# A fused sliding-window attention and mixture-of-experts kernel: one layout of the keys' blocks and its masks against another, with copies and routing steps on other engines

## The chip, the cores and the metric

The kernel runs on one core of one Trainium2 chip. The metric is the device time of one execution in microseconds (us). The kernel before was timed three times: median 500.73 us, from 499.25 to 502.19.

## What is computed

Attention first: batch 4, 8 heads, 768 positions, head size 64. A query sees the 4 first keys of its sequence (the "sinks") and the keys up to 127 positions behind it. Its result, 3072 rows of 512, goes through a mixture of experts: each row takes its best of 4 groups, then its best of that group's 4 experts, and gets that expert's output (512 to 1024, ReLU, 1024 to 512) times two softmax weights. Shortened:

```python
rel = pos[:, None] - pos[None, :]
keep = (pos[None, :] < n_sink) | ((rel >= 0) & (rel < window))     # 4 and 128
a = softmax(where(keep, q @ k.T / sqrt(64), -1e9)) ;  x = rows(a @ v)   # [3072, 512]
g = argmax(x @ w_group) ;  e = argmax(x @ w_expert[g])
out = softmax(x @ w_group)[g] * softmax(x @ w_expert[g])[e] * (relu(x @ w1[g, e]) @ w2[g, e])
```

## The kernel before, in words

*Tiles.* The attention works on 24 tiles of 128 queries (`NI`), six for each batch element (`NT`); all 8 heads of a tile in two groups `g` of four. The main loop (L1209) is a pipeline: iteration `i` makes the scores of tile `i`, weighs the values of tile `a = i-1`, and brings tile `b = i-2` into its natural layout, norms it and makes its routing logits. After the loop come the experts (to 497 us), which the change doesn't touch.

*One tile.* `scores` (L746): TensorE (PE) multiplies each half of 64 queries (on its own half of the partitions) with three blocks of 64 keys, its own and the two before it, each with the 4 sink keys, into the PSUM tile `ps`. With a window of 128 the oldest and the newest block are both needed in part, and in complementary parts: above the diagonal the one, below it the other. The kernel "folds" them: `maxima` (L768) copies by a mask `selu` (a predicated copy) the oldest block's scores over the places of the newest block that lie in the future, so that two blocks of 64 remain, and then runs four instructions of 128x136 per group on VectorE (DVE) that scale, add the mask `msk` and take the row's maximum (`sm`, `st`). `exps` (L783) makes the exponentials `pt` on ScalarE (ACT). `trans` (L797) transposes them on PE into the PSUM tile `tp` (`tp2` in the code), 8 instructions a group, each group in its own columns (`256 * g`); `evac` (L806) copies a group with one ACT instruction of 128x512 to `pw`; `halves` (L812) takes the fold apart again on GpSimd (POOL): two products of the folded quarter with two triangular 0/1 masks `tri`. `values` (L848) multiplies with the value blocks into `po`. The sinks go apart: `sink_copy` (POOL), `sink_t` (PE), `sink_evac` (ACT, `spT`), `sink_values` (PE). Tiles with `t = 0` (the first of a batch element) have no older keys, and neither fold nor masks.

*The two tiles behind.* `out_evac` (L857) copies `po` to `xT` (ACT), `natural` (L861) transposes it into `nat`, other columns of the same PSUM tile (so the trace calls it `po` too), `norm` (L873) divides by the row sums (`xt<-po,rc` on DVE) and writes the tile to memory. `logits` (L867) multiplies `xT` with the routers' weights, into spare columns of the first `ps` tile, and `norm_logits` (L883) takes them out (`lw` on DVE): only then can the next `scores` write there.

*Routing.* `route_batch` (L356) turns the logits of a batch of six tiles (`BATCHES`) into tables, in some 20 steps; each `yield` is a step's end, `yield "pe"` comes ahead of matmuls, `yield "rd"` ahead of reading their result. The main loop takes steps between the attention's instructions through `unit`, `UNITS` (L59) says how many a tile: four in tile 7, seven in tile 8, six in most others, so the batches of tiles 0 to 5, 6 to 11 and 12 to 17 are worked off in the attention, the last one behind it. `on` is POOL in the attention, DVE behind it.

*Order.* Every instruction goes through `_Eng`, which keeps each engine's instructions in the order written. So each trace row bears that helper's line, L105, and rows are told apart by their tile names. PE's weight loads (PEld) run beside its matmuls. The experts' weights are split into two parts in the gaps of the attention (`whi` on ACT, `wlo` on DVE).

```python
L772  v.copy_predicated(psb[g][:, :, SW + NSK:3 * BW], selu..., psb[g][:, :, NSK:BW])      # maxima, t > 0
L776  v.tensor_tensor_reduce(sm[:, k], psb[g][:, k, BW + s:3 * BW + s], msk[:, min(t, 2), s:SW + s], ...)
L809  nc.scalar.copy(pw[:, 0:8]..., tp2[:, :, 256 * g:256 * (g + 1)]...)                  # evac
L816  nc.gpsimd.tensor_tensor(pw[:, 8 * k:8 * k + 4], pw[:, 0:4], tri[:, k, None, :]...)  # halves, k = 1, 0
```

Of the kernel before, what the change touches and what calls it, by code (L numbers as in the profile page):

```python
# [37 lines left out]
SW = 2 * BW  # L38
# [96 lines left out]
def moe_attention(tc, kqT, vN, vS, nsw, wgx, w1, w2, out):  # L135
    nc = Pinned(tc)
    v = nc.vector
    with ExitStack() as top, ExitStack() as att:
# [117 lines left out]
        isu = gp.tile([P, D], F32, name="xg")  # L256
        v.tensor_scalar(isu, dq, 0.0, None, ALU.is_lt)
        rel = gp.tile([P, D], F32, name="xg")
        v.scalar_tensor_tensor(rel, isu, float(P), dq, ALU.mult, ALU.add)
        msk = const([P, 3, MW], F32, "msk")  # L260
        mb, ms, mc = msk[:, :, NSK:BW], msk[:, :, BW:BW + NSK], msk[:, :, BW + NSK:SW]
# [3 lines left out]
        v.tensor_scalar(m4[:, 0, ::SW // NSK], col[:, None, 0:NSK].to_broadcast([P, 2, NSK]), 0.0, NEG, ALU.is_ge, ALU.mult)  # L265
        selu = const([P, D], I32, "selu")
        v.tensor_scalar(selu, dq, 0.0, None, ALU.is_lt)
        dqd = const([P, D], F32, "dqd")
        v.tensor_scalar(dqd, dq, float(D), None, ALU.add)
# [10 lines left out]
        v.tensor_scalar(mc[:, 2], rel, win, NEG, ALU.is_ge, ALU.mult)  # L280
        v.tensor_scalar(snk, col[:, 0:D], nsk, NEG, ALU.is_lt, ALU.mult)
        v.tensor_scalar(mb[:, 2], dqd, win, NEG, ALU.is_ge, ALU.mult)
        v.scalar_tensor_tensor(mc[:, 0], isu, NEG, mc[:, 2], ALU.mult, ALU.add)
# [5 lines left out]
        tri = const([P, 2, D], F32, "tri")  # L289

        def other_masks():
            v.tensor_scalar(tri[:, 0], dq, 0.0, None, ALU.is_le)
            v.tensor_scalar(tri[:, 1], dq, 0.0, None, ALU.is_gt)
            v.tensor_copy(m4[:, 2, ::BW // NSK], m4[:, 0, ::BW // NSK])
            v.tensor_copy(msk[:, 1], msk[:, 2])
            v.tensor_tensor(snk[0:D], snk[0:D], isu[0:D], ALU.mult)
            v.tensor_tensor(mc[0:D, 1], mc[0:D, 1], snk[0:D], ALU.add)
# [58 lines left out]
        def route_batch(i0, nb, lt, wk, pt, tab, na, pick=None):  # L356
# [19 lines left out]
            v.tensor_tensor(d, lv, wide(m), ALU.subtract)  # L376
            yield
# [10 lines left out]
            v.tensor_tensor(oh.rearrange("p n (g e) -> p n g e", g=G), o5[:, :, 1:],  # L388
# [26 lines left out]
            v.tensor_tensor(runb, runb, rs, ALU.add)  # L415
# [18 lines left out]
            v.tensor_tensor(m, og, s5[:, :, 1:], ALU.mult)  # L434
            yield
# [13 lines left out]
            for j0 in range(0, nb, 3):  # L449
# [5 lines left out]
                v.tensor_tensor(af[:, j0:j1], oh[:, j0:j1, :, None].to_broadcast([P, w, NE, na]),  # L455
# [290 lines left out]
        def scores(i, g):  # L746
            t = i % NT
            if g == 0:
                env[i] = e = {}
                e["pt"] = wk.tile([P, HP, 2, 2, BW], F32, name="pt", bufs=2)  # L750
# [17 lines left out]
        def maxima(i, g, between=lambda k: None):  # L768
            t = i % NT
            e = env[i]  # L770
            if t:
                v.copy_predicated(psb[g][:, :, SW + NSK:3 * BW], selu[:, None, :].to_broadcast([P, 4, D]), psb[g][:, :, NSK:BW])  # L772
            between(0)
            e["sm", g] = sm = wk.tile([P, 4, SW], F32, name="sm", bufs=2)
            for k in range(4):
                h, s = head(g, k), k % 2 * NSK  # L776
                v.tensor_tensor_reduce(
                    sm[:, k], psb[g][:, k, BW + s:3 * BW + s], msk[:, min(t, 2), s:SW + s], -0.125, 3.0e38,
                    ALU.add, ALU.min, e["st"][:, h:h + 1])
                if k % 2:  # L780
                    between(k)

        def exps(i, g, ks=range(4)):  # L783
            e = env[i]
            for k in ks:
                h = head(g, k)
                nc.scalar.activation(e["pt"][:, 2 * g + k // 2, :, k % 2], e["sm", g][:, k].rearrange("p (b k) -> p b k", b=2),
# [8 lines left out]

        def trans(i, g):  # L797
            pt = env[i]["pt"].rearrange("p m b l x -> p m b (l x)")
            for j in range(2):
                for k in range(2):  # L800
                    o = 256 * g + (2 * k + j) * D
                    for f in range(2):
                        r = slice(f * D, (f + 1) * D)
                        nc.tensor.transpose(tp2[:, f, o:o + D], pt[r, 2 * g + j, 1 - k, NSK:SW - NSK], ident[r, r])
# [13 lines left out]

        def sink_copy(i):
            src = env[i]["pt"].rearrange("p m b l x -> p m (b l x)")[:, :, SW - NSK:SW + NSK]  # L820
# [3 lines left out]
        def sink_t(i):  # L824
            for f in range(2):
                r = slice(f * D, (f + 1) * D)
                nc.tensor.transpose(tp2[:, f, 0:D], sp[i % 2][r], ident[r, r])

        def sink_evac(i):
            env[i]["spT"] = spT = wk.tile([P, P], F32, name="spT", bufs=2)  # L830
            nc.scalar.copy(spT.rearrange("p (f q) -> p f q", f=2), tp2[:, :, 0:D])
# [82 lines left out]
        def routing(k, kinds=(None, "pe", "rd")):  # L914
            while k > 0:
                if not rb or not have.issuperset(rb[0][0]):
                    return False
                kind = rb[0][2] if isinstance(rb[0][2], str) else None
                if kind not in kinds or (kind == "pe" and state["clk"] < state["at"]):
# [283 lines left out]
        def unit(k):  # L1203
            if quota[0] > 0 and routing(1, (None,)):
# [4 lines left out]
        for i in range(NI + 2):  # L1209
# [15 lines left out]
            if mid:  # L1225
                evac(a, 0)
# [4 lines left out]
            if live:  # L1231
# [4 lines left out]
                warm(FILL[i] if i < len(FILL) else 0, tp2[:, 0, 256:448])  # L1236
            if mid:
                sink_copy(a)
                halves(a, 0)
# [12 lines left out]
            if mid:  # L1252
                evac(a, 1)
# [3 lines left out]
            if mid and not live:  # L1257
                halves(a, 1)
# [12 lines left out]
            if live:  # L1271
                maxima(i, 1, unit)
# [346 lines left out]
```

## Time and profile before

| what | value |
|---|---|
| median of three runs | 500.73 us (499.25 to 502.19) |
| the profiled execution | 499.12 us; its span 497.3 us |
| busy, share of the span | PE 466.5 us (94%), PEld 396.2 (80%), DVE 347.0 (70%), ACT 326.1 (66%), POOL 170.3 (34%) |
| chain that ended last, by engine | PE 65%, DVE 11%, ACT 9%, issue 8%, POOL 4%, DMA 2% |
| of it, by tile | PE `po` 29%, PE `ph` 29%, ACT `pt` 5%, PE `tp` 4%, PE `ps` 3%, POOL `pw` 2% |

The span runs from the first instruction to the last; the time holds a little more, what lies around it. Busy time counts an engine's instructions, and a busy engine need not be the one that all wait for. The chain is followed back from the last instruction to whatever released each. `po`, `tp` and `ps` are the attention's PSUM tiles (`po` and `ph` are the experts' as well), `pt` its exponentials, `pw` its transposed weights. The shares are means over two parts with different limits, the attention and the experts, so stretches have to be read apart.

### The profile page before, as it was taken

What the parts mean: (1) busy time and instruction counts of PE and PEld (TensorE: products, weight loads), DVE (VectorE), ACT (ScalarE), POOL (GpSimd) and SP (SyncE); (2) the same over time, 40 slices, a digit from 0 to 9 for tenths busy, and PEclk for the clock granted to TensorE, in tenths of its full rate; (3) what the DMA queues carried; (4) which work ended last, traced back from release to release, by engine and by line L of the source; (5) the groups of instructions that cost most, each with busy time, mean ns of one, the idle gap of its engine ahead of it and who ended that gap; (6) DMA issues with size and microseconds to landing.
All of it is one profiled execution on the core that took longest, in us unless ns stands there. A gap on an engine that the chain in (4) does not pass through costs nothing.

```text
span 497.3 us, 15548 instructions
## 1 busy us (share of the span) xinstructions
PE 466.5 (94%) x5865; PEld 396.2 (80%) x5865; DVE 347.0 (70%) x1147; ACT 326.1 (66%) x875; POOL 170.3 (34%) x303
## 2 busy tenths in 40 slices
PE   7999889988788998999999999999999999999995
PEld 6788778767667877889897967897879788877894
DVE  6677877897895777796137334844688888787870
ACT  4899779788774332575147247663878877687861
POOL 3565674583766002414020205120503071204021
PEclk9999999999998998999999999999999999999999
DMA  6566557476765529689215277986978997858200
GB/s 192 174 204 217 166 171 214 155 223 213 222 191 162 180 85 355 230 240 373 91 48 150 60 253 239 370 292 229 327 293 298 408 388 273 315 186 332 66 25 30
DMA packets 49556, 107.47 MB, mean 216 GB/s; under 512 B 8932, under 2 KB 9444, under 8 KB 49472
## 3 DMA queue, kind: packets, MB, share of 16 engines
q1 hardware_dynamic: 45008, 93.17, 56.0%
q0 software_dynamic: 4320, 12.94, 7.3%
q8 instruction: 48, 0.79, 0.7%
q10 hardware_dynamic: 144, 0.28, 0.2%
q14 instruction: 36, 0.29, 0.2%
HBM read 93.58 MB, written 12.93 MB: 214 GB/s over the span
## 4 chain that ended last, share of the span: by engine, by line
PE 65%; DVE 11%; ACT 9%; issue 8%; POOL 4%; DMA 2%; POOLq 0%; SPq 0%; DVEq 0%; ACTq 0%
PE po L105 29%; PE ph L105 29%; ACT pt L105 5%; PE tp L105 4%; PE ps L105 3%; POOL pw L105 2%; DVE wlo L105 2%; ACT pw L105 2%; DVE sm L105 1%; DVE xt L105 1%; ACT whi L105 1%; DMA qb<-in_kqT 1%; DVE ps L105 1%; POOL out L105 1%; DVE req L105 1%
## 5 line engine op out<-in xcount | busy, mean ns | idle before, releaser
L105 DVE TENSOR_TENSOR wlo<-rw,whi 128x1024 fp32r<-128x1024 f32 (+1 forms) x116 | 135.8, 1196 | 29.0 <-ACT whi L105 28.4
L105 PE MATMUL ph<-un,whi 128*128 128x256 f32 (+9 forms) x576 | 128.6, 313 | 0.0
L105 PE MATMUL po<-whi,un 128*128 128x512 f32 (+6 forms) x384 | 127.4, 397 | 0.0
L105 POOL DMA_INDIRECT out<-ot,sidx x33 | 41.0, 1244 | 225.4 <-ACT ot L105 169.6
L105 ACT CAST whi<-rw 128x1024 fp32r<-128x1024 f32 (+1 forms) x116 | 114.7, 1018 | 3.4 <-PE po L105 2.3
L105 PE MATMUL ph<-un,wlo 128*128 128x160 f32 (+10 forms) x416 | 99.5, 264 | 0.9 <-DVE wlo L105 0.9
L105 PEld LDWEIGHTS ph<-un,whi 128*128 128x128 f32 x576 | 93.8, 189 | 2.3 <-issue 1.0
L105 PEld LDWEIGHTS po<-whi,un 128*128 128x128 f32 (+5 forms) x384 | 70.6, 185 | 19.7 <-issue 2.1
L105 ACT ACTIVATE pt<-sm,st 128x136 f32<-128x136 f32 x192 | 76.3, 404 | 11.6 <-DVE st L105 11.4
L105 PE MATMUL po<-wlo,un 128*128 128x512 f32 (+7 forms) x200 | 78.7, 393 | 2.2 <-DVE wlo L105 2.2
L105 PEld LDWEIGHTS ph<-un,wlo 128*128 128x128 f32 x416 | 76.8, 189 | 1.5 <-DVE wlo L105 1.1
L105 POOL TENSOR_TENSOR pw<-pw,tri 128x256 f32<-128x256 f32 x80 | 60.1, 752 | 16.2 <-ACT pw L105 12.7
L105 DVE CUSTOM_DVE_ANT_0 sm<-ps,msk 128x136 f32<-128x136 f32 x192 | 46.9, 294 | 6.2 <-PE ps L105 1.1
L105 PE MATMUL po<-pw,vv 64*64 64x128 f32 (+1 forms) x1408 | 40.9, 252 | 9.9 <-POOL pw L105 6.2
L105 PEld LDWEIGHTS po<-pw,vv 64*64 64x64 f32 x1408 | 35.1, 135 | 17.8 <-POOL pw L105 8.5
L105 POOL DMA_INDIRECT xg<-xd,gidx x33 | 35.6, 1077 | 33.6 <-DVE idz L105 16.1
L105 PEld LDWEIGHTS po<-wlo,un 128*128 128x128 f32 (+6 forms) x200 | 36.0, 180 | 10.6 <-DVE wlo L105 2.6
L105 PE MATMUL ps<-kb,qb 64*64 64x204 f32 (+1 forms) x768 | 41.4, 330 | 2.7 <-DVE lw L105 2.2
L105 DVE TENSOR_TENSOR hc<-ph,hc 128x160 f32<-128x160 f32 (+6 forms) x64 | 21.4, 336 | 27.6 <-ACT hc L105 27.6
L105 ACT ACTIVATE un<-ph 128x256 fp32r<-128x256 f32 (+1 forms) x40 | 15.4, 384 | 35.7 <-PE ph L105 35.2
L105 ACT ACTIVATE ot<-po,cg 128x512 f32<-128x512 f32 (+7 forms) x25 | 17.0, 681 | 31.8 <-PE po L105 31.7
L105 ACT ACTIVATION_READ_ACCUMULATOR pt<-sm,st 128x1 f32 x192 | 37.2, 194 | 0.0
(200 smaller groups left out, 659.5 us busy)
## 6 DMA issues: line engine op xcount, KB each, us to landing
rw<-in_w SPq DMA_DIRECT2D x128, 512.0 KB, 5.5
kb<-in_kqT SPq DMA_DIRECT2D x23, 272.0 KB, 4.1
qb<-in_kqT SPq DMA_DIRECT2D x24, 256.0 KB, 3.5
vv<-in_vN SPq DMA_DIRECT2D x24, 256.0 KB, 3.5
xd<-xt SPq DMA_DIRECT2D x24, 256.0 KB, 2.4
xg<-xd,gidx POOLq DMA_INDIRECT x33, 5.9
out<-ot,sidx POOLq DMA_INDIRECT x33, 5.8
sv<-in_vS SPq DMA_DIRECT2D x4, 128.0 KB, 4.9
```

The lines of the kernel that those rows point to most:

```text
L105: r = f(*a, **k)
```

## The change

*Masks and blocks.* The keys are no longer folded. `SW` grows from two blocks to three, `msk` gets a part for the oldest block (`mo`), and `maxima` adds the masks of all three; its four instructions a group are 128x204 (128x136 in tiles with `t = 0`, which begin at `lo`). The predicated copies, `selu`, `tri` and `halves` go, and with them POOL's two products a group. `exps` makes three blocks. *Transposes.* `trans` makes 12 instead of 8 a group (8 with `t = 0`). Both groups now use the same columns 0 to 383 of `tp2`, the sinks 384 to 447; so a group's transposes wait until the other group's copies have read. *Copies.* `evac` is split by the two halves `f` of the queries: `f = 0` on ACT, `f = 1` on DVE, 128x384 each. Group 0's both stand at the iteration's start; of group 1, ACT's stands behind the exponentials of the next tile's first group, DVE's behind the maxima of its second. *Order.* `logits(b)` comes before `values(a, 0)`. *Routing.* Five kinds of step go from `v` to `on`: the subtraction `rdt`, the product `oh`, the sum `runb`, the product `rm` and the tables' `af`. Behind `rdt` and `rm` stands a new `yield "po"`, upon which `unit` skips one turn. The warming matmuls of the first tiles write to other columns.

```diff
-SW = 2 * BW
+NBL = 3
+SW = NBL * BW
...
-        mb, ms, mc = msk[:, :, NSK:BW], msk[:, :, BW:BW + NSK], msk[:, :, BW + NSK:SW]
+        mo, mb = (msk[:, :, x + NSK:x + BW] for x in (0, BW))
+        ms, mc = msk[:, :, 2 * BW:2 * BW + NSK], msk[:, :, 2 * BW + NSK:SW]
...
         def other_masks():
-            v.tensor_scalar(tri[:, 0], dq, 0.0, None, ALU.is_le)
-            v.tensor_scalar(tri[:, 1], dq, 0.0, None, ALU.is_gt)
+            v.tensor_tensor(mc[:, 2], mc[:, 2], isn, ALU.add)
+            v.tensor_scalar(mo[:, 2], dqd[:, 1], win, NEG, ALU.is_ge, ALU.mult)
...
-            v.tensor_tensor(d, lv, wide(m), ALU.subtract)
-            yield
+            on.tensor_tensor(d, lv, wide(m), ALU.subtract)
+            yield "po"
...
-            v.tensor_tensor(oh.rearrange("p n (g e) -> p n g e", g=G), o5[:, :, 1:],
+            on.tensor_tensor(oh.rearrange("p n (g e) -> p n g e", g=G), o5[:, :, 1:],
...
-            v.tensor_tensor(runb, runb, rs, ALU.add)
+            on.tensor_tensor(runb, runb, rs, ALU.add)
...
-            v.tensor_tensor(m, og, s5[:, :, 1:], ALU.mult)
-            yield
+            on.tensor_tensor(m, og, s5[:, :, 1:], ALU.mult)
+            yield "po"
...
-                v.tensor_tensor(af[:, j0:j1], oh[:, j0:j1, :, None].to_broadcast([P, w, NE, na]),
+                on.tensor_tensor(af[:, j0:j1], oh[:, j0:j1, :, None].to_broadcast([P, w, NE, na]),
...
-            if t:
-                v.copy_predicated(psb[g][:, :, SW + NSK:3 * BW], selu[:, None, :].to_broadcast([P, 4, D]), psb[g][:, :, NSK:BW])
+            lo = 0 if t else BW
...
-                    sm[:, k], psb[g][:, k, BW + s:3 * BW + s], msk[:, min(t, 2), s:SW + s], -0.125, 3.0e38,
+                    sm[:, k, lo:], psb[g][:, k, lo + s:SW + s], msk[:, min(t, 2), lo + s:SW + s], -0.125, 3.0e38,
...
+        def kinds(i):
+            return NBL if i % NT else NBL - 1
+
         def trans(i, g):
...
-                for k in range(2):
-                    o = 256 * g + (2 * k + j) * D
+                for k in range(kinds(i)):
+                    o = (2 * k + j) * D
...
-        def evac(i, g):
+        def evac(i, g, f):
             e = env[i]
-            e["pw", g] = pw = wk.tile([P, 12, D], F32, name="pw", bufs=2)
-            nc.scalar.copy(pw[:, 0:8].rearrange("p (m f) q -> p f m q", f=2),
-                           tp2[:, :, 256 * g:256 * (g + 1)].rearrange("p f (m q) -> p f m q", q=D))
-
-        def halves(i, g):
-            pw = env[i]["pw", g]
-            if i % NT:
-                for k in (1, 0):
-                    nc.gpsimd.tensor_tensor(pw[:, 8 * k:8 * k + 4], pw[:, 0:4],
-                                            tri[:, k, None, :].to_broadcast([P, 4, D]), ALU.mult)
+            if f == 0:
+                e["pw", g] = wk.tile([P, 12, D], F32, name="pw", bufs=2)
+            n = 2 * kinds(i)
+            (v.tensor_copy if f else nc.scalar.copy)(e["pw", g][:, f:2 * n:2], tp2[:, f, 0:n * D].rearrange("p (m q) -> p m q", q=D))
...
         def unit(k):
-            if quota[0] > 0 and routing(1, (None,)):
+            if rb and rb[0][2] == "po":
+                rb[0][2] = None
+            elif quota[0] > 0 and routing(1, (None,)):
                 quota[0] -= 1
...
             if mid:
-                evac(a, 0)
+                evac(a, 0, 0)
+                evac(a, 0, 1)
...
             if mid:
                 sink_copy(a)
-                halves(a, 0)
...
             if mid:
-                evac(a, 1)
                 sink_evac(a)
             if live:
                 exps(i, 0, (2, 3))
-            if mid and not live:
-                halves(a, 1)
+            if mid:
+                evac(a, 1, 0)
...
             if live:
                 maxima(i, 1, unit)
+            if mid:
+                evac(a, 1, 1)
             if old:
                 natural(b)
+                logits(b)
             state["clk"] += 3.0
             if live and mid:
                 values(a, 0)
-            if old:
-                logits(b)
...
             if live:
-                if mid:
-                    halves(a, 1)
                 exps(i, 1)
                 trans(i, 0)
```

*Three places in the order of the engines.* DVE, at the end of a tile's second maxima (`sm`, `st`; the rows `st` are the second part of the instruction above them), where `rc`, `lw` and a batch's first routing steps (`row`) follow; before:

```order
L105 ISA sm,st<-ps_211,msk 128x136
L105 ISA st 128x1
L105 TENSOR_REDUCE rc<-sacc_188 128x16
L105 RECIPROCAL rc<-rc 128x16
L105 TENSOR_TENSOR lw<-ps_210,rc 128x160
L105 COPY row<-rev 128x4
L105 TENSOR_REDUCE row<-lt 128x30
```

and with the change:

```order
L106 ISA sm,st<-ps_207,msk 128x204
L106 ISA st 128x1
L106 COPY pw<-tp 128x6x64
L106 TENSOR_REDUCE rc<-sacc_184 128x16
L106 RECIPROCAL rc<-rc 128x16
L106 TENSOR_TENSOR lw<-ps_206,rc 128x160
L106 COPY row<-rev 128x4
L106 TENSOR_REDUCE row<-lt 128x30
```

The second group's copy `pw<-tp` now stands between its last maxima and `rc`.

DVE, the stretch right behind it, with the routing steps `rdt`, `req` and `oh` and the beginning of the next tile's maxima; before:

```order
L105 TENSOR_TENSOR xt<-po,rc 128x2x4x64
L105 TENSOR_TENSOR rdt<-lt,row 128x30x4
L105 SCALAR_TENSOR_TENSOR req<-rdt,row 128x120
L105 TENSOR_REDUCE row<-req 128x30
L105 TENSOR_TENSOR req<-req,row 128x120
L105 TENSOR_TENSOR oh_2186<-req 128x96
L105 COPY_PREDICATED ps_210<-selu,ps_210 128x4x64
L105 ISA sm,st<-ps_210,msk 128x136
L105 ISA st 128x1
```

and with the change:

```order
L106 TENSOR_TENSOR xt<-po,rc 128x2x4x64
L106 SCALAR_TENSOR_TENSOR req<-rdt,row 128x120
L106 TENSOR_REDUCE row<-req 128x30
L106 TENSOR_TENSOR req<-req,row 128x120
L106 COPY pw<-tp 128x6x64
L106 ISA sm,st<-ps_206,msk 128x204
L106 ISA st 128x1
```

`rdt` and `oh` are gone from DVE, the predicated copy too, and the first group's copy stands ahead of the maxima.

PE, in the middle of an iteration: the sinks' and group 1's transposes (`tp<-ident`), the transposes of `natural` (`po<-ident,xT`), group 0's `values` (`po<-pw,vv`) and `logits` (`ps<-wsd,xT`), with the engines that each waits for (the numbers are counts of the semaphores); before:

```order
L105 MATMUL tp<-ident,sp_133 128x64 [waits Activation_49,Pool_49]
L105 MATMUL tp<-ident,sp_133 128x64
L105 MATMUL tp<-ident,pt 128x64 x8
L105 MATMUL po<-ident,xT 128x64 [waits Activation_49]
L105 MATMUL po<-ident,xT 128x64 x7
L105 MATMUL po<-pw,vv 64x128 [waits DMAHW6_49,Pool_49]
L105 MATMUL po<-pw,vv 64x128 x3
L105 MATMUL po<-pw,vv 64x64 x4
L105 MATMUL po<-pw,vv 64x128 x4
L105 MATMUL po<-pw,vv 64x64 x4
L105 MATMUL ps_210<-wsd,xT 64x40 [waits DVE_49]
```

and with the change:

```order
L106 MATMUL po<-ident,xT 128x64 [waits Activation_49]
L106 MATMUL po<-ident,xT 128x64 x7
L106 MATMUL ps_206<-wsd,xT 64x40 [waits DVE_49]
L106 MATMUL ps_206<-wsd,xT 64x40 x7
L106 MATMUL po<-pw,vv 64x128 [waits DMAHW6_49]
L106 MATMUL po<-pw,vv 64x128 x3
L106 MATMUL po<-pw,vv 64x64 x4
L106 MATMUL po<-pw,vv 64x128 x4
L106 MATMUL po<-pw,vv 64x64 x4
L106 MATMUL po<-spT,sv 128x128 [waits Activation_49]
L106 MATMUL po<-spT,sv 128x128 x3
L106 MATMUL tp<-ident,pt 128x64 [waits DVE_49]
```

`logits` now stands ahead of `values`; `values` no longer waits for POOL, and the next tile's transposes of group 0 (the last row) wait for DVE, whose copy reads the columns that they write. The sinks' and group 1's transposes now stand ahead of the piece shown.

## Rows read from the trace of the kernel before

**Rows 1.** Windows: stretch, its us, then PE, PEld, DVE, ACT, POOL busy, PEclk, DMA, GB/s

```profile
25.00:48.00 23.00, 22.83 (x625) 19.51 (x628) 16.23 (x85) 21.14 (x90) 13.60 (x30) 1.00 0.65 209
...
48.00:149.00 101.00, 87.53 (x2271) 72.54 (x2263) 84.76 (x424) 80.89 (x325) 63.48 (x128) 1.00 0.63 196
...
151.00:155.00 4.00, 3.88 (x54) 3.43 (x56) 1.30 (x3) 1.62 (x3) 2.10 (x4) 0.57 0.59 143
```

**Rows 2.** Timeline of ACT: start, us, what; once per tile

```profile
22.24 0.59 ACT L105 COPY xT<-po 128x512 f32<-128x512 f32 x1 [0.85 <-PE po L105]
...
48.17 0.58 ACT L105 COPY xT<-po 128x512 f32<-128x512 f32 x1
...
152.67 0.59 ACT L105 COPY xT<-po 128x512 f32<-128x512 f32 x1 [1.98 <-PE po L105]
```

**Rows 3.** Waits from 15 to 160 us: total us, times, longest

```profile
PE po L105 <- POOL pw L105: 6.2, 11, 2.1
...
DVE ps L105 <- PE ps L105: 4.7, 10, 1.5
```

**Rows 4.** Timeline of PE in a light tile

```profile
22.91 0.41 PE L105 MATMUL tp<-ident,pt 64*128 64x64 f32 x8
...
23.17 0.42 PE L105 MATMUL po<-ident,xT 64*128 64x64 f32 x8
```

**Rows 5.** Timeline of DVE in two heavy tiles, and ahead of 151 us

```profile
55.14 0.42 DVE L105 COPY_PREDICATED ps<-selu,ps 128x256 f32<-128x256 int32 x1
...
55.70 0.30 DVE L105 CUSTOM_DVE_ANT_0 sm<-ps,msk 128x136 f32<-128x136 f32 x1
...
60.93 0.42 DVE L105 COPY_PREDICATED ps<-selu,ps 128x256 f32<-128x256 int32 x1
...
61.27 0.30 DVE L105 TENSOR_REDUCE row<-rdt 128x30 f32<-128x150 f32 x1
...
149.83 0.68 DVE L105 TENSOR_TENSOR xt<-po,rc 128x512 f32<-128x512 f32 x1
```

**Rows 6.** Groups of DVE by shape, 15 to 150 us: busy us, mean ns, idle before

```profile
L105 DVE TENSOR_TENSOR xt<-po,rc 128x512 f32<-128x512 f32 x22 | 15.1, 684 | 3.0 <-PE po L105 1.7 <-ACT pt L105 0.9 <-issue 0.2
...
L105 DVE TENSOR_TENSOR lw<-ps,rc 128x160 f32<-128x160 f32 x22 | 7.1, 322 | 7.2 <-POOL pw L105 3.8 <-PE ps L105 3.0
...
L105 DVE TENSOR_TENSOR runb<-runb,rs 128x16 bf16<-128x16 bf16 x3 | 0.5, 166 | 0.0
```

**Rows 7.** Tiles row, req, rm, af to 170 us: ns min/median/max, first and last start

```profile
L105 DVE COPY row<-rev x4: 165/602/606, 51.8 to 168.2; 128x4 f32<-128x4 f32 x4
...
L105 DVE SCALAR_TENSOR_TENSOR req<-rdt,row x4: 283/695/1042, 53.4 to 168.9; 128x120 f32<-128x120 f32 x4
...
L105 DVE TENSOR_TENSOR rdt<-lt,row x4: 265/276/284, 53.1 to 168.6; 128x120 f32<-128x120 f32 x4
...
L105 DVE TENSOR_TENSOR oh<-req x4: 257/293/297, 54.9 to 169.8; 128x96 bf16<-128x96 f32 x4
...
L105 DVE TENSOR_TENSOR rm<-req,row x3: 215/704/745, 61.9 to 145.8; 128x24 f32<-128x24 f32 x3
...
L105 DVE TENSOR_TENSOR af<-oh,av x6: 497/551/607, 64.4 to 158.8; 128x336 fp32r<-128x336 bf16 x6
```

**Rows 8.** Groups of POOL by shape, to 170 us

```profile
L105 POOL TENSOR_TENSOR pw<-pw,tri 128x256 f32<-128x256 f32 x80 | 60.1, 752 | 16.2 <-ACT pw L105 12.7 <-DVE st L105 0.3
...
L105 POOL TENSOR_TENSOR cw<-rss 128x96 f32<-128x96 f32 x3 | 1.0, 346 | 2.5 <-DVE rss L105 2.5
```

**Rows 9.** Timeline of PE: first and last of five waits for masks

```profile
49.94 0.34 PE L105 MATMUL po<-pw,vv 64*64 64x128 f32 x4 [0.60 <-POOL pw L105]
...
151.12 1.50 PE L105 MATMUL po<-pw,vv 64*64 64x128 f32 x32 [2.15 <-POOL pw L105]
```

**Rows 10.** Groups of ACT by shape, 15 to 150 us

```profile
L105 ACT COPY pw<-tp 128x512 f32<-128x512 f32 x44 | 25.2, 572 | 1.1 <-DVE tab L105 0.9
...
L105 ACT COPY spT<-tp 128x128 f32<-128x128 f32 x22 | 5.9, 268 | 0.0
```

More of the change, by code (lines that the diff above doesn't have):

```diff
@@ L255, in moe_attention @@
             v.tensor_copy(dq[r:r + D], diff[r:r + D, r:r + D])
[L256 to L259, printed above, removed]
+        isn = gp.tile([P, D], F32, name="xg")
+        v.tensor_scalar(isn, dq, 0.0, NEG, ALU.is_lt, ALU.mult)
         msk = const([P, 3, MW], F32, "msk")
-        mb, ms, mc = msk[:, :, NSK:BW], msk[:, :, BW:BW + NSK], msk[:, :, BW + NSK:SW]
+        mo, mb = (msk[:, :, x + NSK:x + BW] for x in (0, BW))
+        ms, mc = msk[:, :, 2 * BW:2 * BW + NSK], msk[:, :, 2 * BW + NSK:SW]
         m4 = msk.rearrange("p v (n k) -> p v n k", k=NSK)
@@ L264, in moe_attention @@
         v.tensor_scalar(mb[0:D, 0], dq[0:D], 0.0, NEG, ALU.mult, ALU.add)
[L265 to L269, printed above, removed]
+        v.tensor_scalar(m4[:, 0, ::BW // NSK], col[:, None, 0:NSK].to_broadcast([P, NBL + 1, NSK]), 0.0, NEG, ALU.is_ge, ALU.mult)
+        dqd = const([P, 2, D], F32, "dqd")
+        for k in range(2):
+            v.tensor_scalar(dqd[:, k], dq, float((k + 1) * D), None, ALU.add)
         warm(WARM, tp2[:, 0, 0:192])
@@ L279, in moe_attention @@
         snk = gp.tile([P, D], F32, name="xg")
-        v.tensor_scalar(mc[:, 2], rel, win, NEG, ALU.is_ge, ALU.mult)
+        v.tensor_scalar(mc[:, 2], dq, win, NEG, ALU.is_ge, ALU.mult)
         v.tensor_scalar(snk, col[:, 0:D], nsk, NEG, ALU.is_lt, ALU.mult)
-        v.tensor_scalar(mb[:, 2], dqd, win, NEG, ALU.is_ge, ALU.mult)
-        v.scalar_tensor_tensor(mc[:, 0], isu, NEG, mc[:, 2], ALU.mult, ALU.add)
+        v.tensor_scalar(mb[:, 2], dqd[:, 0], win, NEG, ALU.is_ge, ALU.mult)
+        v.tensor_tensor(mc[:, 0], mc[:, 2], isn, ALU.add)
         v.tensor_tensor(mb[D:P, 0], mb[D:P, 2], snk[D:P], ALU.add)
@@ L749, in scores @@
                 env[i] = e = {}
-                e["pt"] = wk.tile([P, HP, 2, 2, BW], F32, name="pt", bufs=2)
+                e["pt"] = wk.tile([P, HP, NBL, 2, BW], F32, name="pt", bufs=2)
                 if i % 2 == 0:
@@ L826, in sink_t @@
                 r = slice(f * D, (f + 1) * D)
-                nc.tensor.transpose(tp2[:, f, 0:D], sp[i % 2][r], ident[r, r])
+                nc.tensor.transpose(tp2[:, f, 6 * D:7 * D], sp[i % 2][r], ident[r, r])
         def sink_evac(i):
             env[i]["spT"] = spT = wk.tile([P, P], F32, name="spT", bufs=2)
-            nc.scalar.copy(spT.rearrange("p (f q) -> p f q", f=2), tp2[:, :, 0:D])
+            nc.scalar.copy(spT.rearrange("p (f q) -> p f q", f=2), tp2[:, :, 6 * D:7 * D])
         def quarters(g, c, n, lhs, rhs, start=False, stop=False):
@@ L918, in routing @@
                 kind = rb[0][2] if isinstance(rb[0][2], str) else None
+                kind = None if kind == "po" else kind
                 if kind not in kinds or (kind == "pe" and state["clk"] < state["at"]):
```

14 lines of the change are left out of this document (7 added, 7 removed).

## The prediction

> **What bounds the kernel now.** I read the busy time by stretch first, then the copies that mark each tile, then the engines' rows inside a tile. The attention part is the first 165 us of the profiled execution, whose span is 497.3 us and whose time is 499.12 us. The change touches nothing behind it, so everything is decided there, and what it gains or loses I carry to the end one to one, because the next stage starts from the last tile's output.
>
> Two stretches differ [rows 1]. From 25 to 48 us TensorE (PE) is busy 22.83 of 23.00 us. From 48 to 149 us no engine is full: PE 87.5 of 101, VectorE (DVE) 84.8, ScalarE (ACT) 80.9. The copy `xT<-po` runs once per tile and gives the pace [rows 2]: from 22.24 to 48.17 us five tiles pass at 5.19 us each, and from there to 152.67 us sixteen at 6.53 us each. The slower ones are those in which DVE also works through routing steps; with batches of six tiles and four to seven steps a tile I count 13 such "heavy" tiles and 8 "light" ones. So a light tile is bound by PE, and in a heavy one DVE's list is the longest, with short waits of PE for POOL and of DVE for PE between [rows 3].
>
> **The change, term by term** (minus is a gain).
>
> *More transposes.* Eight transposes take 0.26 us from start to start [rows 4], 0.032 us each. Each tile but the first of a batch gets eight more, so PE has 0.26 us more. In 8 light tiles that is all on the path: **+2.1**. In heavy tiles PE has slack, 13.5 us in 101 [rows 1], and I cost it at nothing; if that cover goes it costs 13 x 0.26 = 3.4.
>
> *DVE inside a tile.* Removed: two predicated copies. The next instruction starts 0.56 us after one where it needs its result and 0.34 us after one where it does not [rows 5]; I take 0.45 each, -0.90. Added: eight maxima are 68 columns longer. From 160 to 512 columns read from PSUM the duration goes from 0.322 to 0.684 us [rows 6], 1.03 ns a column, so 0.07 each and +0.56. Added: two copies of 384 columns. On the same line they last 0.55 us; DVE starts its next instruction 0.08 us before the end (60.93 + 0.42 against 61.27) [rows 5], so 0.47 each and +0.93. Net +0.59 a tile; 13 heavy tiles: **+7.7**. The copy has no row of its own. From below its price is that of the predicated copy of 256 columns, 0.34; from above that of the 512-column instruction, 0.60. I keep 0.47, between the two by columns. The first copy of a tile stands ahead of the maxima, where DVE today waits for the scores, 4.7 us in ten places [rows 3]. A third of that lies in heavy tiles: **-1.5**. In light tiles DVE has 6.8 of 23 us free [rows 1], so its additions cost nothing there.
>
> *Steps moved to POOL.* Per batch `rdt` 0.28, `oh` 0.29, `rm` 0.55 (mean of 0.215, 0.704 and 0.745), two `af` of 0.55 and `runb` 0.17 leave DVE [rows 6, 7], 2.4 us, less 0.05 for each of six because neighbours overlap: 2.1. Three batches: **-6.3**. The fourth runs behind the attention and stays on DVE. What could be given back: DVE has to wait for `rdt` and `rm`. On POOL 96 columns last 0.35 and 256 columns 0.75 [rows 8], so `rdt` lasts about 0.4 and `rm` less. Behind `rdt` DVE has `xt` (0.68) to do, and behind `rm` two maxima of 0.3, so I cost it at nothing here and as a rival below.
>
> *Waits of DVE behind POOL.* The same routing instruction has very different durations [rows 7]: `row<-rev`, four columns, 0.165 at its shortest and 0.602 in the middle; `req<-rdt` 0.283 to 1.042. Their shortest is the one behind the attention, where POOL does no masks. POOL's masks are 60.1 us [rows 8] and go. Three copies of 0.44 and an excess of 0.41, 0.41 and 0.76 come to **-2.9**. The ends are 0 and that. A rule of the Trainium skill stands against taking it all. SBUF — State Buffer, section "SBUF: two separate sides", says that VectorE and GpSimd share one port pair under an exclusive lock, held for a whole instruction, and that VectorE needs it when it has two SBUF inputs while GpSimd reads SBUF. By that rule the steps put on POOL would hold it in turn, and the term would be nearer to 0, the whole sum -2.3 instead of -5.2. The rows agree that masks and slow routing go together; that other POOL work does the same no row here shows.
>
> *PE's waits for POOL.* Five times PE stands still for a mask: 0.60 us at 49.94, the last 2.15 us at 151.12, the four before it 2.34 together [rows 9]. Without masks `po` follows the two copies directly. Of the last I take 0.5, since PE there also needs `xt` from DVE, which starts at 149.83 and lasts 0.68 [rows 5, 6]: **-2.8**, with ends 0 and -4.5. Behind that gap the granted clock is 0.57 for 4 us [rows 1], a mix of its two levels, 1.2 and 2.4 GHz, after two microseconds in which PE did nothing. That costs 0.43 x 4 = 1.7 us of PE time. Now the transposes ahead of the gap wait for DVE's second copy, so PE is idle in two shorter pieces, and I take **-1.5**; the other end is 0.
>
> *ACT.* From 512 to 128 columns a copy from PSUM goes from 0.572 to 0.268 us [rows 10], 0.79 ns a column. Eight exponentials get 0.43 us longer, two copies 0.20 shorter: +0.23 a tile. ACT is not full in either stretch: nothing, covered by 2 and 20 us of idle time. `logits` before `values` adds no instruction and lets `lw` start earlier, behind which the next scores wait. The masks built once before the loop are one instruction fewer; `sm` and `pt` grow but keep their two buffers: nothing.
>
> Sum: 2.1 + 7.7 - 1.5 - 6.3 - 2.9 - 2.8 - 1.5 = **-5.2 us**. The profiled execution lies 1.6 us below the median of the three times shown, 500.73, so I apply the sum to that median: **495.5 us**.
>
> **The rivals.**
>
> *A: another engine is next.* The heavy tiles are not DVE's but a ring of short waits, as no engine is full in them [rows 1]. Then DVE's terms cancel and PE's transposes count in all tiles: +2.1 + 3.4, with -2.8 and -1.5 kept, +1.2: 501.9 us. For it speaks that DVE is idle 16 of 101 us; against, that tiles with routing take 1.3 us longer, with the same PE work.
>
> *B: slower, by DVE's second copy.* It stands behind the second group's maxima and ahead of `lw`; the transposes wait for the one and the next scores for the other, so it lies in the ring scores, maxima, copy, `lw`, scores. If a copy takes 0.60 and the predicated copies were worth only 0.34 each, DVE pays 0.56 + 1.20 - 0.68 = 1.08 a tile, 14.0 instead of 7.7, and with POOL's new steps in place of the masks there is no -2.9: sum +4.0, 504.7 us. It decides from about 0.99 us a tile, where the sum passes zero with the other terms kept. Against it: 384 columns is nearer to 0.47.
>
> *C: routing on POOL turns into a wait.* DVE waits for `rdt` and `rm` and PE for `oh` and `af`. By the two POOL rows 336 columns last 0.93, so a batch pays 0.4 + 0.2 + 0.93 and four hand-overs of about 0.1: 1.9, three batches 5.8: sum +0.6, 501.3 us. The planner skips one turn after such steps, which speaks against it. A page speaks for it: GPSIMD Engine Reference, "Elementwise — side-by-side cycle accounting" (3.1), has a GpSimd elementwise add at about twice VectorE's time. Here 96 columns are 0.346 on POOL against 0.293 for `oh` on DVE, so the trace has less of a gap at this size.
>
> **How the numbers follow.** The forecast gets 0.56, A 0.20, B 0.14, C 0.10. The forecast's own range is 490 to 500: below, the copy at 0.34 (-3.4 more), all of PE's waits (-1.7 more) and of the clock (-0.2 more), -10.5 in all; above, neither the port term nor the clock, -0.8. Taking in A and C and leaving out most of B, 8 times in 10 it lies in **490 to 503 us**. A measurement of this kernel tells about 0.5% (2.5 us) from no change. Faster by more: the forecast but for its upper end, and little of the others, 0.58. Within: the rest of it, most of A and C, 0.26. Slower: B, and some of A, 0.16.
>
> **What would show it.** Right: `pw<-tp` on DVE at 0.5 to 0.6 us; light tiles at 5.4 to 5.5 us, heavy ones near 6.0; `row<-rev` near 0.17 to 0.3; no PE wait on POOL's `pw`; full clock around 151 us. Wrong: heavy tiles at 6.5 us or more, with PE's transposes waiting on DVE; `req` waiting on POOL; or heavy tiles shorter but the stage behind 165 us starting no earlier.

## The result and the profile after

The changed kernel takes **507.16 us** (median of four runs, 505.62 to 507.23), the kernel before beside it 499.99 (four runs). The ratio is **1.0133, 95% interval 1.0087 to 1.0179**: slower by 1.3%, where 495.5 us was forecast and 490 to 503 was the range. The profiled execution took 507.18 us with a span of 505.4.

The same copy as in [rows 2], `xT<-po` on ACT, marks the tiles in the changed kernel (timeline of ACT):

```profile
24.03 0.59 ACT L106 COPY xT<-po 128x512 f32<-128x512 f32 x1 [0.98 <-PE po L106]
...
52.50 0.59 ACT L106 COPY xT<-po 128x512 f32<-128x512 f32 x1 [0.22 <-ACT pw L106]
...
161.51 0.59 ACT L106 COPY xT<-po 128x512 f32<-128x512 f32 x1
```

The five light tiles between the first two marks take 5.69 us each where they took 5.19, the sixteen behind them 6.81 where they took 6.53. At the last mark the changed kernel is 8.8 us late, and its span is 8.1 us longer: the loss is all in the attention, and the stage behind carries it almost one to one, as the prediction said it would. The light tiles lose 0.50 us each, the mix behind them 0.28; another 1.8 us is lost ahead of the first mark. The stretches of [rows 1] (columns as there):

```profile
25.00:48.00 23.00, 22.06 (x611) 18.71 (x606) 17.06 (x85) 19.47 (x80) 4.07 (x16) 1.00 0.58 189
48.00:149.00 101.00, 86.76 (x2241) 71.38 (x2239) 79.84 (x377) 79.16 (x308) 25.22 (x78) 1.00 0.59 188
151.00:155.00 4.00, 4.00 (x70) 3.63 (x72) 3.39 (x15) 3.58 (x13) 1.02 (x4) 0.57 0.02 4
```

In 101 us PE, DVE and ACT are all busy a little less than before: no engine has become the bound. What has come in its place is a wait. Two groups from the waits of the changed kernel (15 to 165 us, columns as in [rows 3]):

```profile
DVE pw L106 <- ACT pw L106: 20.3, 29, 1.6
...
PE tp L106 <- DVE pw L106: 6.3, 11, 1.0
```

DVE stands still 20.3 us, in 29 places, until ACT's copy of the *other* half is done; PE's transposes in turn wait 6.3 us for DVE's copies. One light tile shows it, from the timelines of ACT, DVE and PE (36 to 42 us), engine by engine:

```profile
38.35 0.46 ACT L106 COPY pw<-tp 128x384 f32<-128x384 f32 x1
```

```profile
38.84 0.56 DVE L106 COPY pw<-tp 128x384 f32<-128x384 f32 x1 [1.04 <-ACT pw L106]
39.31 0.31 DVE L106 TENSOR_TENSOR lw<-ps,rc 128x160 f32<-128x160 f32 x1
```

```profile
36.52 0.54 PE L106 MATMUL tp<-ident,pt 64*128 64x64 f32 x12
...
39.45 0.59 PE L106 MATMUL tp<-ident,pt 64*128 64x64 f32 x12
```

The transposes that both copies read (PE, 36.52) end at 37.06. DVE is idle from 37.8 on and could copy its half at once. It starts at 38.84, just behind ACT's copy, and PE's next transposes at 39.45, just behind DVE's. So the two halves, which were to run side by side, run in a row, and here both lie in the ring, that is in the circle of waits that sets the tile's time. The chain of waits followed back through this stretch (34 to 48 us) says the same, with no more than 0.04 us between the pieces:

```profile
37.54 0.91 ACT pt L106 x4
38.45 0.37 ACT pw L106
38.81 0.02 issue
38.84 0.57 DVE pw L106
39.41 0.04 issue
39.45 0.59 PE tp L106 x12
```

In all 48 pairs DVE's copy starts 0.38 us or more after ACT's, and no pair overlaps.

The rest went nearly as written down. Tiles `row` and `req` on DVE, and the steps now on POOL (to 170 us, columns as in [rows 7]):

```profile
L106 DVE COPY row<-rev x3: 159/160/160, 57.0 to 136.7; 128x4 f32<-128x4 f32 x3
...
L106 DVE SCALAR_TENSOR_TENSOR req<-rdt,row x3: 281/283/284, 57.9 to 138.5; 128x120 f32<-128x120 f32 x3
...
L106 POOL TENSOR_TENSOR rdt<-lt,row x3: 400/403/667, 57.4 to 137.8; 128x120 f32<-128x120 f32 x3
...
L106 POOL TENSOR_TENSOR af<-oh,av x6: 780/793/807, 70.3 to 162.4; 128x336 fp32r<-128x336 bf16 x6
```

### The profile page after: what moved, and what is told of

It reads as the page before. It is cut to its first block, busy times and chain, and to the rows that moved or that the text cites. A ratio compares the mean times of both kernels' runs of the same rounds, so it can differ in the third digit from the quotient of the medians.

```text
span 505.4 us, 15746 instructions
## 1 busy us (share of the span) xinstructions
PE 471.8 (93%) x6025; PEld 399.6 (79%) x6025; DVE 351.5 (70%) x1135; ACT 330.1 (65%) x875; POOL 116.8 (23%) x241
## 4 chain that ended last, share of the span: by engine, by line
PE 58%; DVE 16%; ACT 12%; issue 8%; DMA 2%; POOL 1%; SPq 1%; POOLq 0%; DVEq 0%; ACTq 0%
PE ph L106 26%; PE po L106 25%; ACT pt L106 7%; PE tp L106 5%; DVE pw L106 3%; DVE sm L106 3%; DVE wlo L106 2%; PE ps L106 2%; ACT pw L106 2%; DVE xt L106 1%; ACT whi L106 1%; DVE un L106 1%; DMA ni<-in_nsw 1%; POOL out L106 1%; DMA xg<-xd,gidx 1%
## 5 line engine op out<-in xcount | busy, mean ns | idle before, releaser
L106 ACT ACTIVATE pt<-sm,st 128x204 f32<-128x204 f32 (+1 forms) x192 | 85.6, 451 | 10.9 <-DVE st L106 8.5
L106 DVE CUSTOM_DVE_ANT_0 sm<-ps,msk 128x204 f32<-128x204 f32 (+1 forms) x192 | 56.1, 352 | 0.7 <-DVE msk L106 0.2
L106 POOL DMA_INDIRECT xg<-xd,gidx x33 | 35.6, 1078 | 37.8 <-DVE idz L106 16.2
L106 DVE COPY pw<-tp 128x384 f32<-128x384 f32 (+1 forms) x48 | 25.6, 533 | 21.7 <-ACT pw L106 21.7
```

The lines of the kernel that those rows point to most:

```text
L106: r = f(*a, **k)
```

## The experiments

**Two PSUM tiles for the transposes.** The rows show that DVE waits, not why: its half lies in other columns of `tp`, in the second of the tile's two banks, and nothing that ACT writes is read by it. The lists of instructions name the engines that each copy waits for (the 49 is part of the semaphores' names, not a count, here as in the lists ahead of the prediction); here DVE's copies in two iterations, group 1's and group 0's in turn, first in the changed kernel, then with one tile per half:

```
105 L106 COPY pw<-tp 128x6x64 [waits PE_49,Activation_49]
108 L106 COPY pw<-tp 128x6x64 [waits Activation_49]
125 L106 COPY pw<-tp 128x6x64 [waits DVE_49,PE_49,Activation_49]
130 L106 COPY pw<-tp 128x6x64 [waits Activation_49]

105 L106 COPY pw<-tp_97 128x6x64 [waits Activation_49]
108 L106 COPY pw<-tp_97 128x6x64 [waits DVE_49,PE_49]
125 L106 COPY pw<-tp_97 128x6x64 [waits DVE_49,Activation_49]
130 L106 COPY pw<-tp_97 128x6x64 [waits PE_49]
```

With one tile, every copy waits for ACT. With two, group 0's waits for PE and in one case for earlier work of DVE itself; what group 1's still waits for on ACT is the sinks' copy from the same tile, which comes earlier. So the order is put there when the program is built: the two engines that read this one PSUM tile are put one behind the other. (A tile of its own for DVE's half of the destination `pw`, with the one tile `tp` kept, leaves the wait for ACT in the list.)

```diff
-        tp2 = ps_p.tile([P, 2, 512], F32, name="tp")
+        tpx = [ps_p.tile([P, 512], F32, name=f"tp{f}") for f in range(2)]
...
-            nc.scalar.copy(spT.rearrange("p (f q) -> p f q", f=2), tp2[:, :, 6 * D:7 * D])
+            for f in range(2):
+                nc.scalar.copy(spT[:, f * D:(f + 1) * D], tpx[f][:, 6 * D:7 * D])
```

> The changed kernel with the transposes' PSUM tile as two tiles of one bank each, one per half of the queries, so that DVE's copy of its half need not wait for ACT's copy of the other; the sinks' ACT copy becomes two of 64 columns. Theory 1 (the two copies run one behind the other because they read one tile; in the changed kernel's trace DVE's copy waits 20.3 us in 29 places for ACT's): those waits go, a light tile falls from 5.69 us to about 5.3, a heavy one by about 0.4, 24 tiles by 0.4: about 10 us, near 498 us. Theory 2 (the waits only stand in for the shared place of both groups: the transposes wait for ACT's late copy anyway): less than 2 us, 505 to 507. Theory 3 (DVE's own load sets the heavy tiles): light tiles gain 0.4 each, heavy ones nothing: about 503 to 504.

Measured: 498.43 us (12 runs), ratio 0.9935 (0.9909 to 0.9961) to the kernel before. Against the changed kernel that is 0.9935 / 1.0133 = 0.980, some 9.8 us of 500 (about 7 to 12, with the intervals of both). No wait of DVE for ACT's copies is left. Light tiles fall to (48.32 - 22.07) / 5 = 5.25 us (timeline of ACT):

```profile
22.07 0.58 ACT L106 COPY xT<-po 128x512 f32<-128x512 f32 x1 [0.53 <-ACT pw L106]
...
48.32 0.59 ACT L106 COPY xT<-po 128x512 f32<-128x512 f32 x1
```

DVE's copy now often comes first:

```profile
29.47 0.55 DVE L106 COPY pw<-tp 128x384 f32<-128x384 f32 x1
```

```profile
30.04 0.47 ACT L106 COPY pw<-tp 128x384 f32<-128x384 f32 x1
```

(timelines of DVE and of ACT, 27 to 34 us). Where both run at once, as at 56.04 (DVE, 0.55 us) and 56.21 (ACT, 0.46), neither is longer than alone. Twelve of 48 pairs overlap by over 0.15 us; in others DVE is up to 1.03 us ahead, or up to 2.73 us behind. So the gain is as much that DVE need not wait for ACT's place in its list as that the copies overlap. Theory 1 is shown; theories 2 and 3 fall.

**One copy at a time.** The rival B of the prediction blamed the second group's copy alone. Two kernels keep one tile and put one group's copy whole on ACT, the second group's (shown) and, as its mirror, the first's:

```diff
+            if g == 1:
+                if f == 0:
+                    nc.scalar.copy(e["pw", g][:, 0:2 * n].rearrange("p (m f) q -> p f m q", f=2), tp2[:, :, 0:n * D].rearrange("p f (m q) -> p f m q", q=D))
+                return
```

> The changed kernel (one PSUM tile) with the second group's copy whole on ACT (128x768) and only the first group's still split and one behind the other. Rival B of the prediction put the cost in the second group's copy on DVE (ring scores, maxima, copy, lw, scores): then this takes most of the 8.7 us back that two tiles gave, 499 to 501. If both copies cost alike, half of it: 502 to 504. If the first group's is the one, 505 or more.

> The mirror of it: the first group's copy whole on ACT, the second group's still split and one behind the other. If the second group's copy carries the cost: 504 to 507. If both alike: 502 to 504. If the first group's does: 499 to 501.

Measured: 504.34 us, ratio 1.0074 (1.0048 to 1.0099), and 504.32 us, ratio 1.0070 (1.0046 to 1.0093). Each takes back about 3 us of the changed kernel's loss. In us the two lie at 504.3, just above the 502 to 504 that stood for "both alike"; taken as ratios to the 499.99 us beside the changed kernel they are 503.7 and 503.5. The two agree with each other, so both copies cost alike, and rival B's ring has no more of the loss than the ring through the first copy. (Both copies on ACT, the next experiment, give back 9.6 us, more than the sum of the two.) The wait that is left, of the first kernel and of the second (waits, 15 to 165 us):

```profile
DVE pw L106 <- ACT pw L106: 17.7, 17, 2.2
```

```profile
DVE pw L106 <- ACT pw L106: 16.5, 18, 1.4
```

**Both copies on ACT.** One instruction of 128x768 a group, none on DVE.

> The changed kernel with one ACT copy of 128x768 per group in the place of ACT's two of 128x384 and none on DVE. Theory 1: one copy of about 0.75 us takes the place of two in a row (0.95 us from start to end of both), so the ring through the transposes is 0.2 us shorter per copy, and DVE has 1 us less per tile: about 497 to 502 us. Theory 3 (DVE's load, of which the copies are 0.95 us a tile): 13 heavy tiles gain 0.9 each, about 495. If ACT becomes the bound (0.6 us more per tile; it was idle 22 of 101 us): no gain or slower, 507 or more.

Measured: 499.06 us, ratio 0.9941 (0.9917 to 0.9964), as fast as the split over two tiles. The copies by tile `pw` (ns min/median/max):

```profile
L106 ACT COPY pw<-tp x48: 563/792/836, 11.3 to 153.9; 128x768 f32<-128x768 f32 x40, 128x512 f32<-128x512 f32 x8
```

0.79 us for the whole is less than 0.46 and 0.56 in a row. In the heavy stretch (columns as in [rows 1])

```profile
48.00:149.00 101.00, 91.82 (x2415) 77.25 (x2413) 73.74 (x383) 92.87 (x330) 28.58 (x92) 1.00 0.63 200
```

DVE's list is 11 us shorter than with two tiles (84.4), and yet the time is the same. DVE's load alone does not set the time, then; but ACT has taken the load over, 92.87 us busy where it was 83.04 with two tiles, so this run does not say what a lighter DVE list is worth with ACT as it was.

**Routing steps, with and without POOL's masks.** Three kernels move the five kinds of step alone: back to DVE in the kernel with two tiles, back to DVE in the changed kernel, and to POOL in the kernel before.

```diff
-            on.tensor_tensor(d, lv, wide(m), ALU.subtract)
-            yield "po"
+            v.tensor_tensor(d, lv, wide(m), ALU.subtract)
+            yield
...
```

> The kernel with two PSUM tiles of before, with the five kinds of routing steps back on DVE (and no skipped turns). The prediction's term says that POOL saves DVE 2.1 us a batch in three batches: if that is on the path, this takes 6.3 us more than with POOL, about 504.5. If the path goes through PE, ACT and hand-overs and DVE has slack, or if what POOL saves is lost in longer steps and waits for them (rdt 0.40 on POOL against 0.28 on DVE, af 0.79 against 0.55), the same within 1.5 us: 497 to 500. If POOL's steps cost more than they save, 495 to 497.

> The changed kernel (one PSUM tile, copies one behind the other) with the five kinds of routing steps back on DVE. With DVE's list on the path and DVE's waits for ACT in it, 2.1 us a batch more: 513. If the waits for ACT's copies leave DVE room (it waits 20.3 us for them), most is hidden: 506 to 509. Slower or faster here than in the kernel with two tiles tells whether the waits and the routing add up.

> The kernel before with only the routing steps on POOL (with the skipped turns). By the prediction's term: -6.3 us if DVE bounds the heavy tiles, so about 494; with the masks still on POOL the steps queue behind them and both may wait: 500 or more. If it gains under 1 us, DVE's list was not the bound of the heavy tiles.

Measured: 498.72 us, ratio 0.9977 (0.9958 to 0.9997), 0.42% above the two tiles with POOL; 509.82 us, 1.0206 (1.0178 to 1.0234), 0.72% above the changed kernel and between its two forecasts; 503.62 us, 1.0039 (1.0012 to 1.0065), slower than the kernel before. So without masks POOL's steps are worth some 2.1 and 3.6 us, not 6.3, with intervals that just touch those of the kernels they are set against; beside the masks they cost 2. One thing that takes a part back is a copy of another kind: the sinks' copy `sp` queues behind the routing steps on POOL, and PE's transposes wait for it. With two tiles, routing on POOL (waits, 15 to 165 us):

```profile
PEld tp L106 <- POOL sp L106: 8.2, 8, 2.7
...
PE tp L106 <- POOL sp L106: 5.0, 4, 2.3
```

and with the same steps back on DVE, where PE's matmuls have no such wait at all:

```profile
PEld tp L106 <- POOL sp L106: 1.3, 3, 0.7
```

The longest of these waits, with two tiles and routing on POOL (timelines of POOL and PE): `oh` stands still on POOL until DVE's `req` is done, `sp` stands behind `oh`, and PE waits 2.30 us for `sp`.

```profile
130.53 0.36 POOL L106 TENSOR_TENSOR oh<-req 128x96 bf16<-128x96 f32 x1 [1.03 <-DVE req L106]
130.83 0.21 POOL L106 COPY sp<-pt 128x32 f32<-128x32 f32 x1
...
131.09 0.28 PE L106 MATMUL tp<-ident,sp 64*128 64x64 f32 x2 [2.30 <-POOL sp L106]
```

In the kernel before with routing on POOL, the masks stand behind it, and DVE's `lw` and PE's values behind the masks (waits, 15 to 165 us; in the kernel before these three are 3.0, 6.2 and 3.8 us); the short copy `row<-rev` stays slow there (tile `row`):

```profile
DVE lw L105 <- PE ps L105: 11.6, 14, 1.9
PE po L105 <- POOL pw L105: 10.1, 16, 0.9
DVE lw L105 <- POOL pw L105: 6.5, 7, 1.8
```

```profile
L105 DVE COPY row<-rev x3: 596/597/602, 53.0 to 131.1; 128x4 f32<-128x4 f32 x3
```

**A third mask product.** The kernel before with its second product done twice.

```diff
-                for k in (1, 0):
+                for k in (1, 0, 0):
```

> The kernel before with its second mask product done twice (the result stays the same), one more POOL instruction of 0.75 us per group and tile, 40 in all. The prediction gave the removal of two such products per group 2.9 (DVE behind POOL) + 2.8 (PE waiting for a mask) + 1.5 (clock): half of it or more should come on top: 4 us or more, 505 and up. If the masks are covered (POOL has slack and PE's waits for them are short), under 1 us: 500 to 502.

Measured: 513.51 us, ratio 1.0274 (1.0248 to 1.0300): 13.7 us for 40 products, 0.34 us of the 0.75 that each lasts. PE's wait for masks goes from 6.2 us [rows 3] to

```profile
PE po L105 <- POOL pw L105: 14.8, 22, 1.5
```

The masks were nowhere near covered. But not all of the 13.7 us is waiting: in the profiled execution the granted clock is low for 16 us of the attention, where before it was for 4 (columns as in [rows 1]).

```profile
136.00:144.00 8.00, 7.47 (x128) 6.51 (x128) 4.38 (x10) 3.88 (x15) 7.08 (x13) 0.57 0.67 228
...
156.00:164.00 8.00, 6.72 (x111) 4.88 (x112) 5.73 (x25) 4.85 (x20) 6.31 (x12) 0.57 0.46 135
```

By these rows 12 us more at 0.57 are an estimate of 0.43 x 12 = 5.2 us, which leaves some 8.5 us, 0.21 a product. What two fewer would give can't be read from one more, and taking them away alone was not tried, as the result would be wrong and with it the routing.

**Logits first.** The kernel before with `logits(b)` ahead of `values(a, 0)`.

> The kernel before with only the logits ahead of the first group's values. The prediction costed this at nothing: 499 to 501. If the next scores wait for the copy out of the logits' columns, up to 0.4 us in tiles where they wait: 497; if the values, now later, delay the output's copy: 502.

Measured: 501.99 us, with 501.18 for the kernel before beside it, ratio 1.0010 (0.9990 to 1.0030): nothing, as costed.

**Versions that beat both.** With two tiles, ACT's copy of group 1 goes back ahead of the sinks' copy and of two exponentials:

```diff
             if mid:
+                evac(a, 1, 0)
                 sink_evac(a)
             if live:
                 exps(i, 0, (2, 3))
-            if mid:
-                evac(a, 1, 0)
```

> The kernel with two PSUM tiles with ACT's copy of the second group back where it stood before the change, ahead of the sinks' copy and of the last two exponentials of the first group. If the transposes of the next tile wait for that copy (1.9 us on PE and its loads in eight places) or DVE is never late, up to 2 us faster: 496.5. If the exponentials behind it come later and with them the transposes, the same or 1 us slower: 498 to 500.

Measured: 496.55 us, ratio 0.9930 (0.9907 to 0.9954), not told apart from 0.9935. But its trace holds the same kind of wait again: the routing's matmuls write into other columns of the same PSUM tile as the transposes, and DVE's read of them (`pe<-tp`), written behind the next tile's transposes, waits for these too. The routing's matmuls end at 57.66, DVE reads at 58.78 (timeline of DVE, 56 to 60 us):

```profile
58.78 0.26 DVE L106 TENSOR_TENSOR pe<-tp,oh 128x96 f32<-128x96 f32 x1 [1.13 <-PE tp L106]
```

So in one more version the read is written ahead of the transposes. The order on PE, DVE, ACT and POOL stays the same; only who waits for whom changes:

```diff
                 exps(i, 1)
+                routing(1, ("rd",))
                 trans(i, 0)
-                routing(1, ("rd",))
```

> The kernel with two PSUM tiles and ACT's earlier copy, with the step that reads the routing's matmuls (pe, tab on DVE) written ahead of the next tile's transposes; no engine's own order changes, but the read no longer waits for transposes that write other columns of the same tile, and the transposes wait for the read. DVE waits there 8.2 us in five places today; where they lie on the path, 2 to 5 us faster: 492 to 495. If the transposes then stand still for DVE instead, no gain: 496 to 498.

Measured: **491.86 us, ratio 0.9821 (0.9799 to 0.9842)**, 1.1% below the version it starts from and 1.8% below the kernel before, and just under the 492 to 495 us expected. DVE now reads at 57.40, with no wait (timeline of DVE, 55 to 60 us); PE is busy 95.38 of the heavy stretch's 101 us, where it was 87.53 [rows 1]:

```profile
57.40 0.26 DVE L106 TENSOR_TENSOR pe<-tp,oh 128x96 f32<-128x96 f32 x1
```

```profile
48.00:149.00 101.00, 95.38 (x2513) 81.81 (x2509) 91.83 (x427) 89.30 (x357) 31.24 (x98) 1.00 0.64 203
```

The same move in the kernel before:

> The kernel before with only that one step moved: the read of the routing's matmuls written ahead of the next tile's transposes. DVE waits there 3.6 us or so in the kernel before (pe and tab, waiting for transposes); if they lie on the path, 1 to 3 us faster: 497 to 499. If the masks on POOL and the waits around them set the heavy tiles there, no gain: 500 to 501. The difference to the gain with two tiles tells how much of that version's gain needs the change.

Measured: 495.50 us, with 499.05 for the kernel before beside it, ratio 0.9934 (0.9911 to 0.9958), some 3.3 us where 1 to 3 were expected. So of the best version's 1.79% the move alone gives 0.66% in the kernel before; the other 1.13% come only with the change in its repaired form. (Counted in the other order, the repaired change gives 0.70% and the move on top of it 1.1%.)

## Why the prediction was wrong

**The step that failed** is the one on DVE inside a tile: "Added: two copies of 384 columns", priced at 0.47 us each, with a gain of 1.5 us because the first one "stands ahead of the maxima, where DVE today waits for the scores". The price was right: the next instruction starts 0.47 us behind the copy's start (38.84 to 39.31). What was left out is that the copy waits for ACT's: the sum has no term for it, so it treats the two halves as independent, and DVE's order was read without the engines that each row waits for; the wait stands in that list. The prediction's own sign of being wrong came: the sixteen tiles behind the light ones at 6.81 us, and PE's transposes waiting on DVE. With the one tile made into two, the rest of the change gives 0.9935, a gain of 3.2 us, inside the range and the forecast's own range. The wait is worth 9.8 us, twice the whole sum. That the rest falls inside the range is in part luck, as the next paragraphs show: terms of both signs were too large, and their errors cancel.

**A reading.** The sixteen tiles at 6.53 us are called slow as a whole; by the prediction's own count three of them are light, so the 13 heavy ones took (104.5 - 3 x 5.19) / 13 = 6.84 us before and (109.0 - 3 x 5.69) / 13 = 7.07 with the change. "Heavy ones near 6.0" and "6.5 us or more" were set against the mix.

**More transposes** (+2.1 in light tiles): right in kind, too dear. With two tiles a light tile takes 5.25 us against 5.19, so 0.06 and not 0.26. The instructions themselves cost nearly what was worked out (with two tiles twelve transposes take 0.37 us from start to start, eight 0.26 [rows 4]: 0.22 a tile). The mean of five takes in the first tile of a batch element, which has only eight; the sum counts such tiles among its eight light ones, too. From one light tile's transposes to those of the next (PE, 28.24 to 33.56 before, 28.17 to 33.64 with two tiles) it is 5.32 and 5.47 us, 0.15 more; what became shorter by the other 0.07 was not traced.

**DVE's terms** (+7.7): the pieces came out as worked: maxima from 0.22 to 0.29 us from start to start, the copy at 0.47. But with both copies on ACT, which takes 0.95 us a tile off DVE, the sixteen tiles take 6.37 us each where they take 6.48 with two tiles: 1.8 us in all for 11 us of DVE's time, with more load on ACT. In this rival A was nearer: the heavy tiles are as much a ring of waits as DVE's list, and a term of DVE's load can't be carried to the end one to one.

**Routing on POOL** (-6.3): 2.1 to 3.6 us. The load leaves DVE as costed; on POOL `rdt` lasts 0.403 us (0.276 on DVE), `af` 0.793 (0.551), and it was right that DVE hardly waits for `rdt` and `rm` (0.3 us in one place in the changed kernel, 2.0 in one place with two tiles). What I had not asked is what is queued behind these steps on POOL: the sinks' copy, for which PE then waits. Rival C looked at the wrong follower.

**DVE behind POOL's masks** (-2.9): the durations fell as written; what that was worth in time no run shows alone. `row<-rev` went from 0.602 to 0.160 us and `req` from 0.695 to 0.283 at the median, the shortest values of before; `rdt` and `rm` left DVE. So the term did not fall to 0. By the rule of the Trainium skill that was weighed there (SBUF — State Buffer, "SBUF: two separate sides") the steps moved to POOL might have held the port in turn. One row, from the kernel before with routing on POOL, agrees with the rule: DVE's routing step `bf`, which has two inputs in SBUF and takes 0.55 us at the median there, lasts 1.15 beside POOL's `af` (timelines of DVE and POOL):

```profile
112.75 1.15 DVE L105 TENSOR_TENSOR bf<-colm,row 128x384 fp32r<-128x384 f32 x1
```

```profile
112.24 2.30 POOL L105 TENSOR_TENSOR af<-oh,av 128x336 fp32r<-128x336 bf16 x2
```

The slow copy `row<-rev` stays at 0.597 where the masks stay; it has one input, so the condition that the prediction quotes does not cover it. `req` falls to 0.280 even there, with `rdt` ahead of it on POOL.

**PE behind POOL's masks** (-2.8): these waits are gone from the list. **The clock** (-1.5): wrong. The granted clock is again 0.57 from 151 to 155 us, the same mix of 1.2 and 2.4 GHz. Ahead of it PE stands still for 1.53 us, now for DVE's maxima (timeline of PE, 149 to 165 us); so there is a gap again, with another cause:

```profile
149.54 0.28 PE L106 MATMUL tp<-ident,sp 64*128 64x64 f32 x2 [1.53 <-DVE st L106]
```

That the gap brings the clock down is not shown. With the second group's copy on ACT the same instruction stands behind the same gap, and the granted clock stays at 1.00 from there to 170 us (timeline of PE):

```profile
146.07 0.28 PE L106 MATMUL tp<-ident,sp 64*128 64x64 f32 x2 [1.53 <-DVE st L106]
```

The low stretch moves from version to version: with two tiles the clock is 0.50 at 132 to 134 us and 1.00 from 151 to 155, and in the profiles with both copies on ACT, with two tiles and routing on DVE, and with the read written first, the attention has none. A stretch like that of [rows 1] is worth 1.7 us of PE's time, so differences of 1 or 2 us between two profiled executions should not be read as the change's. (The gain of the earlier read is not the clock's: the fastest runs without and with it, 494.52 and 490.73 us, have the same mean clock, 0.997.)

**Rival B** named the right side, and a copy on DVE in the ring, but the wrong mechanism: not a copy of 0.60 us, but one of 0.47 that starts too late, and the first copy as much as the second. **ACT** at nothing: its load is not the bound (79.16 us of 101), but its copy, late in its list, is what DVE waits for. **Logits** at nothing: right.

## What to carry to other kernels

Splitting a copy over two engines gains only if both may start together: ask of each new instruction not only how long it lasts but whom it waits for, and look at its list of waits before pricing it. Two engines that read one tile, or a read of columns that nobody overwrites, can be ordered by the tile and not by the data; one tile per reader cost one more short copy on ACT and was worth 2.0% here, a read written ahead of the unrelated write cost nothing and was worth 1.1%. And when a step moves to an idle engine, price what is queued behind it there.

## What the runs showed of the hardware

Two engines reading PSUM at once, from different banks, do not slow each other: DVE's copy of 384 columns lasts 0.55 us and ACT's 0.46 in pairs that overlap (56.04 and 56.21) as in those that don't. The page Advanced Engine Details and Errata of the Trainium skill, section "Bank Collisions", says so too. And one more product of 0.75 us on an engine busy for 63 of 101 us [rows 1] cost 0.34 us each time, 0.21 by the estimate without the lower clock: an engine far from full can still be in the ring. In the same way an instruction of one engine can be stretched by another's: four columns on DVE take 0.60 us beside POOL's masks and 0.16 where they are gone.
